# A spectral mixer with soft experts and a gated layer: constants in four pools, weight loads in another order

## The chip, the cores and the metric

The kernel runs on one NeuronCore of one Trainium2 chip. Time is device time in microseconds (us) of one execution; the median of several executions counts. TensorE (PE; its weight loads are PEld), VectorE (DVE), ScalarE (ACT) and GpSimd (POOL) compute; SyncE (SP) only issues transfers. A name with a q behind it (SPq, ACTq) is the engine's queue of instructions. Transfers that are issued by SyncE, ScalarE or GpSimd run on 16 shared DMA engines.

## The reference

All data are float32, with 8 sequences of 3072 tokens and 256 channels.

```python
X = np.fft.rfft(x, axis=1)                       # x: 8 x 3072 x 256
y = np.fft.irfft(X * (filt_r + 1j*filt_i), n=3072, axis=1)
...
logits = y @ phi                                 # y: 24576 x 256; 8 experts x 4 slots
d = softmax over the tokens (axis 0); slot_in = d.T @ y
slot_out[e] = relu(slot_in[e] @ w1[e]) @ w2[e]   # 256 -> 1024 -> 256, per expert
c = softmax over the slots (axis 1);  z = c @ slot_out
...
g = z @ w_gate; v = z @ w_val                    # 256 -> 1536
out = (g * sigmoid(g) * v) @ w_out               # 1536 -> 256
```

## The kernel before, in words

There are three parts, written out in the order in which each engine runs them; nothing reorders the instructions. `phase1` (0 to about 434 us) goes over the 8 sequences in two halves of the channels: a forward transform in two steps (L211, L242), the product with the filter (L250, L251), and for each sequence a `chain` of steps that gets the logits and their token softmax (L346 to L478). It reads four constants from one pool `big`: `ft` (the filter), `inv` and `fwd` (transform matrices) and `nyq`. Beside it `conv` turns the float64 weights of the gated layer, which arrive as integer pairs, into float32 copies in DRAM: `wd[0]` (gate), `wd[1]` (value), `wd[2]` (output). `first_weights` puts the slot softmax of the first sequence's tokens into DRAM as `cd`.

`transition` (about 404 to 469 us) loads expert weights `w1_e` and `w2_e` (1 MB each) and the gate weights `wg` and `wv` (1.5 MB each) into places in SBUF that phase 1 had used. SBUF is full, so each of these loads waits until the tiles whose place it takes have been read for the last time. Places are given back pool by pool. All are issued from SyncE by `flat_load` (L129), in the order of the text; where one waits, those behind it wait too. The expert layer runs as `stage1` (w1, L745, in calls `stage1(0,0)`, `(0,1)`, `(1,0)` and `(1,1)`, where the first index is the half of the experts), transposes `turn` (L762; the copies ht, L763) and `stage2` (w2, L770; first the experts 0 to 3, then 4 to 7). Its output `so` is turned into `sot` and multiplied with wg and wv (L805 for the first 512 columns, L816 for the rest). That gives `g4_0`, `v4_0` and, through `gh` and `gl` and sixteen small transfers (L828), `g4_1`, `g4_2`, `v4_1`, `v4_2`.

`phase2` (from the first G, L916, to the end) goes over 576 items: 8 sequences x 3 x 2 token groups x 12 blocks `f` of 128 of the 1536 columns. An item multiplies the slot softmax `c4` with g4 (G, L916) and v4 (V, L917), forms silu(G)*V, splits it into a high and a low part, and multiplies both with the output weights `wo[f]` (L944, L948), some items later. The first twelve items also split `wo[f]` into two parts (`load_out`, L905, L906). Items f = 0 to 3 use g4_0, items 4 to 7 g4_1. The first `c4` comes from `cd` in four transfers of 384 KB, each to 32 partitions, and `wo` from `wd[2]` in twelve (`first`, L846 and L852), all on SyncE, called after the last `stage1`.

A transfer by SyncE or ScalarE signals its landing on one of eight semaphores that go round. A transfer waits until the one before it on its semaphore has landed, so at most eight of them are under way.

Of the kernel before, what the change touches and what calls it, by code (L numbers as in the profile page):

```python
# [7 lines left out]
F32 = mybir.dt.float32  # L8
F32R = mybir.dt.float32r
# [8 lines left out]
NB, SEQ, D, E = 8, 3072, 256, 32  # L18
NEXP, SPE, FE, FF = 8, 4, 1024, 1536
NJ, NP, NR = 24, 96, 32  # L20
NF = FF // 128
# [58 lines left out]
def spectral_softmoe_glu_kernel(  # L80
# [17 lines left out]
    nc = tc.nc  # L98
# [16 lines left out]
    wd = [dram.tile([256, FF], F32, name="wgd"), dram.tile([256, FF], F32, name="wvd"), dram.tile([FF, 256], F32, name="wod")]  # L115
# [5 lines left out]
    w1s = {}  # L121

    def one(shape, name, stack=c2, side="left", dt=F32):

        p = stack.enter_context(tc.tile_pool(name=f"p_{name}", bufs=1, side=side))
        return p.tile(shape, dt, tag=name, name=name)

    def flat_load(dst, src, p):
        nc.sync.dma_start(out=dst, in_=src.rearrange("(t p) f -> p t f", p=p))  # L129


    def phase1():
        with ExitStack() as c1:
# [6 lines left out]
            yp = [c1.enter_context(tc.tile_pool(name=f"yp{k}", bufs=1)) for k in range(3)]  # L140
            pq = c1.enter_context(tc.tile_pool(name="pq", bufs=2))
            ytp = c1.enter_context(tc.tile_pool(name="ytp", bufs=3))
            big = c1.enter_context(tc.tile_pool(name="big", bufs=1))
            chp = c1.enter_context(tc.tile_pool(name="chp", bufs=1))
            ps_s1 = c1.enter_context(tc.tile_pool(name="ps_s1", bufs=1, space=PSUM))
            ps_x = c1.enter_context(tc.tile_pool(name="ps_x", bufs=2, space=PSUM))
# [1 line left out]
            ps_l = c1.enter_context(tc.tile_pool(name="ps_l", bufs=1, space=PSUM))  # L148
            ps_c = c1.enter_context(tc.tile_pool(name="ps_c", bufs=1, space=PSUM))

            ft = big.tile([128, 12, 2, D], F32, name="ft")
            inv = big.tile([128, NJ, 128], F32, name="inv")
            fwd = big.tile([128, NJ, 128], F32, name="fwd")
            nyq = big.tile([1, D], F32, name="nyq")

            xt = {}
            bt = {}
# [540 lines left out]
    def transition():  # L698
# [5 lines left out]
        w2s = {}  # L704
# [16 lines left out]
        one([128, 2 * D - 64], "pad2")  # L721
        wg = one([128, 2, FF], "wg")
        wv = one([128, 2, FF], "wv")
        flat_load(w2s[0], w2[0], 128)
        for e in range(4, NEXP):
            flat_load(w1s[e], w1[e], 128)
        for e in (1, 2, 3, 5, 6, 7, 4):
            flat_load(w2s[e], w2[e], 128)
        flat_load(wg, wd[0], 128)
        flat_load(wv, wd[1], 128)  # L730

        pool.memset(stm, 0.0)
# [50 lines left out]
        stage1(1, 1)  # L783
        c3.close()
        later = phase2_tiles()
        later["first"]()
        turn(0, 1)
# [14 lines left out]
        for w, dst in gates:  # L802
            pg = bank([128, 512], "h")
            for d_ in range(2):
                pe.matmul(  # L805
                    out=pg, lhsT=sot[:, d_, :], rhs=w[:, d_, 0:512], start=(d_ == 0), stop=(d_ == 1)
# [7 lines left out]
        for d_ in range(2):  # L814
            for i, (w, n, c) in enumerate(parts):
                pe.matmul(  # L816
                    out=pg[32 * i:32 * i + 32, :],
# [8 lines left out]
        for i, (w, n, c) in enumerate(parts):  # L826
            for r in range(4):
                (nc.sync if r < 2 else nc.gpsimd).dma_start(  # L828
                    out=later[n][c][32 * r:32 * r + 32, :].bitcast(F32),
                    in_=(gl if r % 2 else gh)[32 * i:32 * i + 32, :].bitcast(F32),  # L830
# [5 lines left out]
    def phase2_tiles():  # L836
        cp = p2.enter_context(tc.tile_pool(name="cp", bufs=1, side="right"))
        g4 = [cp.tile([128, 512], F32R, name=f"g4_{c}") for c in range(3)]
        v4 = [cp.tile([128, 512], F32R, name=f"v4_{c}") for c in range(3)]
        wo = [cp.tile([128, 2, D], F32R, name=f"wo{f}") for f in range(NF)]  # L840
        c4 = {}

        def first():
            t = cp.tile([128, 3, 2, 512], F32R, tag="c4", name="c4", bufs=2)
            for r in range(4):
                nc.sync.dma_start(  # L846
                    out=t[32 * r:32 * r + 32].rearrange("p q G n -> p q (G n)").bitcast(F32),
                    in_=cd[r // 2].rearrange("q e n -> e q n"),
                )
            c4[0] = t  # L850
            for f in range(NF):
                nc.sync.dma_start(out=wo[f][:, 1, :].bitcast(F32), in_=wd[2][f * 128:(f + 1) * 128, :])  # L852

        def build(b):
            lg = cp.tile([96, E, 32], F32, tag="lg", name="lg", bufs=2)
# [138 lines left out]
    with tc.manual_schedule():  # L994
        phase1()
        phase2(transition())
        p2.close()
# [32 lines left out]
```

## Time and profile before

| | us |
|---|---|
| median of three runs | 1562.45 (1561.62 to 1564.56) |
| profiled execution, whole | 1558.03 |
| its span, first to last instruction | 1556.2 |
| TensorE busy | 1477.5 (95%) |
| VectorE busy | 1182.4 (76%) |
| ScalarE busy | 954.1 (61%) |
| first instruction of phase 2 (L916) | 469.13 |

The page lists engines by busy time and follows the chain of work that ended last back from the last instruction. The timeline gives start, duration, engine, line, operation and tiles, and in brackets how long the engine had been idle and what ended that. A granted clock of 1.0 is TensorE's 2.4 GHz, 0.5 its 1.2 GHz. Buffer numbers are left out of names in the profile: `w` stands for w1_e and w2_e, `c` for c4, `g` and `v` for g4 and v4.

### The profile page before, as it was taken

What the parts mean: (1) busy time and instruction counts of PE and PEld (TensorE: products, weight loads), DVE (VectorE), ACT (ScalarE), POOL (GpSimd) and SP (SyncE); (2) the same over time, 40 slices, a digit from 0 to 9 for tenths busy, and PEclk for the clock granted to TensorE, in tenths of its full rate; (3) what the DMA queues carried; (4) which work ended last, traced back from release to release, by engine and by line L of the source; (5) the groups of instructions that cost most, each with busy time, mean ns of one, the idle gap of its engine ahead of it and who ended that gap; (6) DMA issues with size and microseconds to landing.
All of it is one profiled execution on the core that took longest, in us unless ns stands there. A gap on an engine that the chain in (4) does not pass through costs nothing.

```text
span 1556.2 us, 26502 instructions
## 1 busy us (share of the span) xinstructions
PE 1477.5 (95%) x10218; PEld 1146.6 (74%) x10218; DVE 1182.4 (76%) x1960; ACT 954.1 (61%) x1808; POOL 238.3 (15%) x300
## 2 busy tenths in 40 slices
PE   4799999999778999999999999999999999999998
PEld 1355555555436888888888888888888888888887
DVE  1597887877528887887797788789788878877775
ACT  1365655644316766766776676677667667666665
POOL 0465555553201000000000010000000000000000
PEclk9799999988999999999999999999999999999999
DMA  9997787782592021112102111211211211120111
GB/s 174 181 163 123 131 138 135 128 120 95 206 319 82 14 68 38 28 42 51 28 19 63 38 28 42 51 28 33 50 38 28 62 31 28 35 61 15 27 28 27
DMA packets 105297, 116.58 MB, mean 75 GB/s; under 512 B 14770, under 2 KB 85172, under 8 KB 104916
## 3 DMA queue, kind: packets, MB, share of 16 engines
q1 hardware_dynamic: 102260, 110.44, 33.8%
q10 hardware_dynamic: 2656, 3.93, 0.9%
q8 instruction: 80, 1.31, 0.4%
q0 software_dynamic: 256, 0.52, 0.1%
q14 instruction: 45, 0.37, 0.1%
HBM read 68.21 MB, written 34.60 MB: 66 GB/s over the span
## 4 chain that ended last, share of the span: by engine, by line
PE 84%; DVE 4%; DMA 4%; SPq 3%; ACT 2%; issue 2%; POOL 0%; ACTq 0%; DVEq 0%; POOLq 0%
PE o L944 34%; PE o L948 17%; PE V L917 9%; PE G L916 9%; PE X L242 4%; PE T L273 3%; PE s L211 2%; DMA c<-cd 1%; PE c L455 1%; SPq L173 1%; SPq L129 1%; PE L L282 1%; PE c L417 1%; DMA raw<-in_moe_w_gate_dram 1%; DVE sg L219 1%
## 5 line engine op out<-in xcount | busy, mean ns | idle before, releaser
L944 PE MATMUL o<-wo,hi 128*128 128x512 f32 x2304 | 832.5, 396 | 0.0
L948 PE MATMUL o<-wo,lo 128*128 128x256 f32 x2304 | 646.6, 281 | 0.2 <-DVE lo L933 0.2
L919 ACT ACTIVATE s<-G 128x512 f32<-128x512 f32 x576 | 344.6, 598 | 320.5 <-PE G L916 317.2
L925 DVE TENSOR_TENSOR h<-V,s 128x512 f32<-128x512 f32 x576 | 394.9, 686 | 171.3 <-ACT s L919 168.8
L944 PEld LDWEIGHTS o<-wo,hi 128*128 128x128 f32 x2304 | 433.4, 188 | 102.9
L948 PEld LDWEIGHTS o<-wo,lo 128*128 128x128 f32 x2304 | 435.2, 189 | 25.4 <-DVE lo L933 0.6
L933 DVE TENSOR_TENSOR lo<-h,hi 128x512 fp32r<-128x512 f32 x576 | 417.0, 724 | 0.1
L932 ACT CAST hi<-h 128x512 fp32r<-128x512 f32 x576 | 354.4, 615 | 14.4 <-DVE h L925 10.2
L916 PE MATMUL G<-c,g 128*128 128x512 f32 x576 | 228.4, 397 | 2.2 <-DMA g<-gl 1.6
L917 PE MATMUL V<-c,v 128*128 128x512 f32 x576 | 227.8, 396 | 2.2 <-DVE h L925 1.7
L242 PEld LDWEIGHTS X<-b,fwd 128*64 128x64 f32 x1536 | 86.9, 143 | 76.7 <-issue 51.7
L275 ACT COPY yt<-T 128x512 f32<-128x512 f32 x96 | 55.9, 583 | 136.3 <-PE T L273 132.8
L916 PEld LDWEIGHTS G<-c,g 128*128 128x128 f32 x576 | 108.5, 188 | 28.2 <-issue 3.4
L219 DVE STREAM_TRANSPOSE sg<-s 128x1024 f32<-128x1024 f32 x64 | 79.4, 1240 | 57.2 <-PE s L211 57.0
L242 PE MATMUL X<-b,fwd 128*64 128x128 f32 x1536 | 110.4, 289 | 11.8 <-ACT b L228 10.3
L917 PEld LDWEIGHTS V<-c,v 128*128 128x128 f32 x576 | 109.0, 189 | 4.0 <-DVE h L925 2.8
L863 POOL TENSOR_TENSOR lg<-lg,mx 96x1024 f32<-96x1024 f32 x7 | 16.8, 2397 | 585.4 <-DVE mx L861 585.4
L211 PE MATMUL s<-x,csm 48*64 48x512 f32 x512 | 84.7, 679 | 22.0 <-DMA x<-in_x_dram 15.2
L958 DVE TENSOR_TENSOR ot<-o,tmp 128x256 f32<-128x256 f32 x192 | 70.1, 423 | 38.4 <-ACT tmp L957 38.4
L263 POOL TENSOR_TENSOR y<-P 128x256 f32<-128x256 f32 x96 | 70.2, 732 | 144.7 <-DVE P L250 144.3
L251 DVE TENSOR_TENSOR Q<-X,ft 128x512 f32<-128x512 f32 x96 | 64.9, 677 | 13.7 <-POOL y L263 13.7
L228 ACT COPY b<-sg 128x768 f32<-128x768 f32 x64 | 58.6, 916 | 26.6 <-DVE sg L219 26.3
(194 smaller groups left out, 1021.1 us busy)
## 6 DMA issues: line engine op xcount, KB each, us to landing
x<-in_x_dram SPq DMA_DIRECT2D x64, 384.0 KB, 8.1
out_dram<-ot SPq DMA_DIRECT2D x192, 128.0 KB, 2.2
w<-in_moe_w_dram SPq DMA_DIRECT2D x16, 1024.0 KB, 9.6
c<-ch SPq DMA_DIRECT2D x42, 128.0 KB, 2.4
c<-cl SPq DMA_DIRECT2D x42, 128.0 KB, 2.4
raw<-in_moe_w_gate_dram SPq DMA_DIRECT2D x12, 256.0 KB, 4.5
lgd<-lg ACTq DMA_DIRECT2D x16, 192.0 KB, 4.4
raw<-in_moe_w_val_dram SPq DMA_DIRECT2D x12, 256.0 KB, 3.5
```

Source lines behind the costliest of these rows:

```text
L211: pe.matmul(out=ps[64 * k:64 * k + 64, 16 * r:16 * r + 16, :], lhsT=s1t_sb[64 * r:64 * r + 48, :], rhs=xt[step][64 * r:64 * r + 48, k, :, ...
L219: dve.transpose(out=sg.rearrange("p j d k -> p d j k"), in_=ps.rearrange("p n d -> p d n"))
L242: pe.matmul(out=ps[par * 64:(par + 1) * 64, i, ri, :], lhsT=fwd[:, j, ri * 64:(ri + 1) * 64], rhs=bb[:, j, :],)
L263: pool.tensor_tensor(out=y[:, :, 0, :], in0=P[:, :, 0, :], in1=P[:, :, 1, :], op=ALU.subtract)
L916: pe.matmul(out=pg, lhsT=g4[c][:, fs], rhs=c4[b][:, q, G, :])
L917: pe.matmul(out=pv, lhsT=v4[c][:, fs], rhs=c4[b][:, q, G, :])
L919: act.activation(s, pg, AF.Silu)
L925: dve.tensor_tensor(out=h, in0=pv, in1=s, op=ALU.mult)
L932: act.copy(hi, h)
L933: dve.tensor_tensor(out=lo, in0=h, in1=hi, op=ALU.subtract)
L944: pe.matmul(out=a, lhsT=hi[:, ts], rhs=wo[f].rearrange("p k d -> p (k d)"), start=(f == 0), stop=(f == NF - 1), skip_group_check=True,)
L948: pe.matmul(out=a[:, D:2 * D], lhsT=lo[:, ts], rhs=wo[f][:, 0, :], start=False, stop=(f == NF - 1), skip_group_check=True,)
```

## The change

The four constants get a pool each. The requests of `transition` stand in another order. The first `c4` is requested half by SyncE and half by ScalarE, and `wo` is held in three tiles of four blocks, filled by one transfer each.

```diff
@@ -140,7 +140,7 @@
             yp = [c1.enter_context(tc.tile_pool(name=f"yp{k}", bufs=1)) for k in range(3)]
             pq = c1.enter_context(tc.tile_pool(name="pq", bufs=2))
             ytp = c1.enter_context(tc.tile_pool(name="ytp", bufs=3))
-            big = c1.enter_context(tc.tile_pool(name="big", bufs=1))
+            big = [c1.enter_context(tc.tile_pool(name=f"big{k}", bufs=1)) for k in range(4)]
             chp = c1.enter_context(tc.tile_pool(name="chp", bufs=1))
             ps_s1 = c1.enter_context(tc.tile_pool(name="ps_s1", bufs=1, space=PSUM))
             ps_x = c1.enter_context(tc.tile_pool(name="ps_x", bufs=2, space=PSUM))
@@ -148,10 +148,10 @@
             ps_l = c1.enter_context(tc.tile_pool(name="ps_l", bufs=1, space=PSUM))
             ps_c = c1.enter_context(tc.tile_pool(name="ps_c", bufs=1, space=PSUM))
 
-            ft = big.tile([128, 12, 2, D], F32, name="ft")
-            inv = big.tile([128, NJ, 128], F32, name="inv")
-            fwd = big.tile([128, NJ, 128], F32, name="fwd")
-            nyq = big.tile([1, D], F32, name="nyq")
+            ft = big[0].tile([128, 12, 2, D], F32, name="ft")
+            inv = big[1].tile([128, NJ, 128], F32, name="inv")
+            fwd = big[2].tile([128, NJ, 128], F32, name="fwd")
+            nyq = big[3].tile([1, D], F32, name="nyq")
 
             xt = {}
             bt = {}
@@ -721,12 +721,17 @@
         one([128, 2 * D - 64], "pad2")
         wg = one([128, 2, FF], "wg")
         wv = one([128, 2, FF], "wv")
+
+        for e in (4, 5):
+            flat_load(w1s[e], w1[e], 128)
         flat_load(w2s[0], w2[0], 128)
-        for e in range(4, NEXP):
+        for e in (6, 7):
             flat_load(w1s[e], w1[e], 128)
-        for e in (1, 2, 3, 5, 6, 7, 4):
+        for e in (6, 7):
             flat_load(w2s[e], w2[e], 128)
         flat_load(wg, wd[0], 128)
+        for e in (1, 2, 3, 5, 4):
+            flat_load(w2s[e], w2[e], 128)
         flat_load(wv, wd[1], 128)
 
         pool.memset(stm, 0.0)
@@ -837,19 +842,24 @@
         cp = p2.enter_context(tc.tile_pool(name="cp", bufs=1, side="right"))
         g4 = [cp.tile([128, 512], F32R, name=f"g4_{c}") for c in range(3)]
         v4 = [cp.tile([128, 512], F32R, name=f"v4_{c}") for c in range(3)]
-        wo = [cp.tile([128, 2, D], F32R, name=f"wo{f}") for f in range(NF)]
+        wo4 = [cp.tile([128, 4, 2, D], F32R, name=f"wo{c}") for c in range(3)]
+        wo = [wo4[f // 4][:, f % 4] for f in range(NF)]
         c4 = {}
 
         def first():
             t = cp.tile([128, 3, 2, 512], F32R, tag="c4", name="c4", bufs=2)
+
             for r in range(4):
-                nc.sync.dma_start(
+                (nc.sync if r < 2 else nc.scalar).dma_start(
                     out=t[32 * r:32 * r + 32].rearrange("p q G n -> p q (G n)").bitcast(F32),
                     in_=cd[r // 2].rearrange("q e n -> e q n"),
                 )
             c4[0] = t
-            for f in range(NF):
-                nc.sync.dma_start(out=wo[f][:, 1, :].bitcast(F32), in_=wd[2][f * 128:(f + 1) * 128, :])
+            for c in range(3):
+                nc.sync.dma_start(
+                    out=wo4[c][:, :, 1, :].bitcast(F32),
+                    in_=wd[2][c * 512:(c + 1) * 512, :].rearrange("(f p) d -> p f d", p=128),
+                )
 
         def build(b):
             lg = cp.tile([96, E, 32], F32, tag="lg", name="lg", bufs=2)
```

In the changed file lines behind L721 stand 5 to 10 further down: `flat_load` is still L129, the ht copies are L768, the c4 requests L853, the wo requests L859 and the small transfers L833.

On SyncE, from the load of w1_6 to that of wv. In the kernel before:

```order
L129 DMA w1_6_4734<-in_moe_w1_dram 128x2x1024
L129 DMA w1_7_4730<-in_moe_w1_dram 128x2x1024
L129 DMA w2_1_5083<-in_moe_w2_dram 128x8x256
L129 DMA w2_2_5087<-in_moe_w2_dram 128x8x256
L129 DMA w2_3_5091<-in_moe_w2_dram 128x8x256
L129 DMA w2_5_5135<-in_moe_w2_dram 128x8x256
L129 DMA w2_6_5139<-in_moe_w2_dram 128x8x256
L129 DMA w2_7_5143<-in_moe_w2_dram 128x8x256
L129 DMA w2_4_5131<-in_moe_w2_dram 128x8x256
L129 DMA wg_5155<-wgd_67 128x2x1536
L129 DMA wv_5159<-wvd_68 128x2x1536
```

The same stretch of SyncE in the changed kernel:

```order
L129 DMA w1_6_4743<-in_moe_w1_dram 128x2x1024
L129 DMA w1_7_4739<-in_moe_w1_dram 128x2x1024
L129 DMA w2_6_5151<-in_moe_w2_dram 128x8x256
L129 DMA w2_7_5155<-in_moe_w2_dram 128x8x256
L129 DMA wg_5167<-wgd_67 128x2x1536
L129 DMA w2_1_5095<-in_moe_w2_dram 128x8x256
L129 DMA w2_2_5099<-in_moe_w2_dram 128x8x256
L129 DMA w2_3_5103<-in_moe_w2_dram 128x8x256
L129 DMA w2_5_5147<-in_moe_w2_dram 128x8x256
L129 DMA w2_4_5143<-in_moe_w2_dram 128x8x256
L129 DMA wv_5171<-wvd_68 128x2x1536
```

w2_6, w2_7 and wg moved ahead of w2_1; wv is still last. The load of w2_0, some rows up, moved behind w1_4 and w1_5.

On ScalarE, where the ht copies stand, between `stage1` and `so`. In the kernel before:

```order
L754 ACTIVATE hs0_5075<-h_5180 128x512
L754 ACTIVATE hs1_5079<-h_5200 128x512
L763 COPY ht00_5095<-t_5210 128x512
L763 COPY ht10_5103<-t_5294 128x512
L794 COPY so_5111<-o_5179 128x256
```

The same place on ScalarE in the changed kernel:

```order
L759 ACTIVATE hs0_5087<-h_5192 128x512
L759 ACTIVATE hs1_5091<-h_5212 128x512
L768 COPY ht00_5107<-t_5222 128x512
L853 DMA c4_5258<-cd_71 32x3x1024 x2
L768 COPY ht10_5115<-t_5288 128x512
L799 COPY so_5123<-o_5191 128x256
```

Two of the four c4 requests now stand between the two ht copies.

## Rows read from the trace of the kernel before

**Rows 1.** Page, part 4: shares of the chain that ended last, by engine
```profile
PE 84%; DVE 4%; DMA 4%; SPq 3%; ACT 2%; issue 2%; POOL 0%; ACTq 0%; DVEq 0%; POOLq 0%
```

**Rows 2.** Chain of waits, 426 to 480: start us, us, what
```profile
447.87 21.13 DMA c<-cd
...
473.25 3.53 DMA v<-gl
```

**Rows 3.** SyncE's own waits: who, for whom, us in total, times, longest
```profile
SPq L129 <- PE cl L455: 20.6, 1, 20.6
```

**Rows 4.** SyncE's timeline, 426 to 472: start us, us, line, operation, tiles, count
```profile
426.13 14.81 SPq L129 DMA_DIRECT2D w<-in_moe_w_dram  x7
...
432.13 5.85 SPq L129 DMA_DIRECT2D w<-in_moe_w_dram  x2
...
446.29 2.01 SPq L846 DMA_DIRECT2D c<-cd  x4
...
448.34 6.93 SPq L852 DMA_DIRECT2D wo<-wod  x3
...
462.00 9.22 SPq L852 DMA_DIRECT2D wo<-wod  x9
```

**Rows 5.** Timeline: last readers of the constants ft, inv and fwd
```profile
405.28 0.68 DVE L251 TENSOR_TENSOR Q<-X,ft 128x512 f32<-128x512 f32 x1
...
412.01 0.62 PE L356 MATMUL cl<-inv,lhb 128*32 128x128 f32 x16
...
425.86 1.54 PE L424 MATMUL cl<-fwd,bd 128*32 128x128 f32 x48
```

**Rows 6.** DMA issues: KB each, median us to landing; the last line is L846's
```profile
w<-in_moe_w_dram SPq DMA_DIRECT2D x1, 1024.0 KB, 13.1
...
lgd<-lg ACTq DMA_DIRECT2D x1, 192.0 KB, 7.5
...
DMA to landing us min/median/max: 17.1/19.1/21.1
```

**Rows 7.** Stretches: engines' busy us, granted clock, DMA share, GB/s
```profile
412.00:426.00 14.00, 10.95 (x147) 6.14 (x143) 7.20 (x14) 4.74 (x11) 0.00 (x0) 1.00 0.10 29
...
426.00:448.00 22.00, 20.11 (x268) 9.57 (x261) 5.12 (x17) 4.80 (x11) 0.53 (x1) 1.00 1.00 318
```

**Rows 8.** TensorE's timeline, 441 to 478; in brackets the idle time before
```profile
441.31 1.92 PE L745 MATMUL h<-w,stm 128*32 128x512 f32 x16
...
451.29 3.66 PE L770 MATMUL o<-w,ht 128*32 128x256 f32 x64 [2.56 <-DMA w<-in_moe_w_dram]
...
456.67 1.98 PE L805 MATMUL h<-wg,sot 128*128 128x512 f32 x4 [0.52 <-DVE sot L799]
...
462.03 3.78 PE L805 MATMUL h<-wv,sot 128*128 128x512 f32 x4 [3.38 <-DMA wv<-wvd]
...
465.74 1.06 PE L816 MATMUL t<-wg,sot 128*32 128x512 f32 x1
...
469.13 0.47 PE L916 MATMUL G<-c,g 128*128 128x512 f32 x1 [0.59 <-DMA c<-cd]
...
475.95 0.47 PE L916 MATMUL G<-c,g 128*128 128x512 f32 x1 [1.62 <-DMA g<-gl]
...
476.91 0.47 PE L917 MATMUL V<-c,v 128*128 128x512 f32 x1 [0.50 <-DMA v<-gl]
```

**Rows 9.** Timeline of ScalarE and SyncE at the copies ht, gh and their transfers
```profile
446.31 0.59 ACT L763 COPY ht<-t 128x512 f32<-128x512 f32 x1 [4.31 <-PE t L762]
...
468.62 0.59 ACT L824 CAST gh<-t 128x512 fp32r<-128x512 f32 x1 [2.18 <-PE t L816]
...
471.33 0.58 SPq L828 DMA_DIRECT2D g<-gh  x1
```

**Rows 10.** Stretches at the lower clock: busy us, granted clock, DMA share, GB/s
```profile
461.00:467.00 6.00, 4.97 (x12) 1.57 (x16) 0.54 (x1) 0.58 (x1) 0.00 (x0) 0.50 1.06 206
...
477.80:481.20 3.40, 3.40 (x12) 2.82 (x11) 1.93 (x5) 1.32 (x4) 0.00 (x0) 0.50 0.32 110
```
## Prediction, made before the changed kernel ran

> **What bounds the kernel now.** Read the page's chain first [rows 1]: TensorE carries 84% of the time from the first to the last instruction, so nothing off TensorE's path can be gained or lost except where TensorE stands still. Nearly all of that 84% is phase 2, which the change leaves as it is. The transfers that the change moves all lie between 404 and 477 us, so the second view is the chain in that stretch: it runs through 21.13 us of a c4 transfer and 3.53 us on a piece of v4 [rows 2]. Third is TensorE's timeline there. It idles 2.56 us for expert output weights before stage 2's second half, 3.38 us for wv, 1.62 us and 0.50 us for pieces of g4 and v4 [rows 8]. Fourth is the cause: SyncE, which issues the loads in order, stands 20.6 us on w2_1, whose place becomes free only with a matmul of L455 [rows 3]. Until it ends at 426.13, w2_2 to w2_7, wg and wv stand behind it [rows 4], and the DMA engines are 10% busy over 412 to 426. Over 426 to 448 they are 100% busy [rows 7]. So TensorE waits for transfers that could have run in an idle stretch 14 us long.
>
> **The requests in a new order, with the constants' pools split.** Once split, a load waits only for the last reader of the constant whose place it takes. By the waits of the two built programs w2_6 and w2_7 now wait for ft, read last by the DVE instruction at 405.28 + 0.68; wg for inv, read last at 412.01 + 0.62; wv for fwd, read last at 425.86 + 1.54 [rows 5]. So 1 + 1 + 1.5 MB are asked for at 406 to 413, ahead of the 20.6 us wait. From 426.13 on five w2 loads and wv remain where there were seven, wg and wv. At the 318 GB/s of 426 to 448 [rows 7], which includes the start-up, the 3.67 million bytes are 11.5 us of DMA work, and the 14 idle us hold them. I take them as landed before 426.
>
> What follows on TensorE, step by step:
> (a) Stage 2's second half. The last w2 load is now the fifth in the queue. The fifth before was issued at 432.13 and landed 13.1 us later, at 445.2 [rows 4, 6]. TensorE wants it at 451.29 - 2.56 = 448.7 [rows 8]. The wait goes: 2.6 us.
> (b) wv. The third wo issue, at the end of the 6.93 us from 448.34, stood on wg's landing, 454.9 [rows 4]; wv landed at 462.0 [rows 8], 7.1 us later beside c4. Now wv follows the fifth w2: 445.2 + 7.1 = 452.3 at that pace, 450.1 at 318 GB/s. It is wanted after wg's matmuls, 456.67 - 2.6 + 1.98 = 456.0 [rows 8]. The 3.38 us go.
> (c) The clock. After that wait TensorE was granted 0.50, its 1.2 GHz level, over 461 to 467 [rows 10]. wv's four matmuls took 3.78 us against 1.98 for wg's same four [rows 8]: 1.8 us. From 465.74 to the first G at 469.13 are 3.39 us, for sixteen matmuls in four rounds of four; at wg's 0.5 us a matmul that is 2.0: 1.4 us, which includes the 0.59 us wait for c4. Without the idle stretch I expect 2.4 GHz: 3.2 us. The first G then stands at 469.13 - 2.6 - 3.4 - 3.2 = 459.9.
>
> **c4 on two queues, wo in three transfers.** Four c4 loads go two to SyncE and two to ScalarE. The shortest and the longest landing, 17.1 and 21.1 us after issues 446.29 and about 447.9 [rows 4, 6], put the four at 463.4 to 469.0, so 1.9 us each. Before, wv and c4 together took 454.9 to 469.0, 14.1 us. The latest now is 445.2 + 14.1 = 459.3; the earliest, with both queues at once, 445.2 + 4.9 + 3.75 = 453.9. Both are under the 459.9 that G asks for, so c4 costs and gains nothing by itself, but the slack can be as little as 0.6 us. The Trainium skill speaks against the second queue: "SBUF — State Buffer", section "Can I just issue two DMAs to hit both halves?", says that two transfers at once, at partition 0 and at partition 64, gained only 6% over a single one. By that rule c4 ends near the later bound, and the rival of a late c4 below gets likelier. No row here has two queues on c4.
>
> ScalarE now issues two transfers between two copies ht, and waits for stage 1's last read, 441.31 + 1.92 = 443.2 [rows 8]. It has been idle for 4.31 us when its next copy starts at 446.31 [rows 9]; four issues took SyncE 2.01 us [rows 4], so two are about 1.0 and end near 444.3. Behind them stands only that copy: nothing lost, and 2 us in hand.
>
> wo becomes three requests of 512 KB instead of twelve of 128. Before, nine of the twelve stood on SyncE from 462.00 for 9.22 us, each until an earlier transfer landed [rows 4], so the first g4 piece was issued at 471.33, though gh was ready at 468.62 + 0.59 = 469.2 [rows 9]. Three requests find their turn early. (d) With gh ready at 460.0, the v4 piece that was issued 1.92 us after the first (473.25) goes at 462.0 and lands 3.53 later [rows 2, 9], at 465.6. TensorE is through its first work at 475.95 - 1.62 = 474.3, 5.2 us after the first G, and so now at 465.1; with the next G the V comes at 465.6 [rows 8]. Of 2.1 us idle I take 2.0 as gained. wo's first third has to land by the time its copy follows the first s, about 461; by bytes (1.65 us at 318 GB/s) it lands at 461 at the latest and 455.6 at the earliest. Per third, copies and matmuls are the same, and no reader of one f waits for the copy of another by the order of the built program: nothing.
> (e) Over 477.8 to 481.2, just after those waits, the clock was at 0.50 again with TensorE busy in all 3.40 us [rows 10]. Without the waits I expect full speed: half of it, 1.7 us.
>
> **The rest.** Up to the first expert load every engine has the same rows in the same order, so the four pools cost nothing in phase 1. DMA beside the end of phase 1 is new at 412 to 422; during it TensorE was 78% busy at full clock without it [rows 7]. Bounds for that, plus the two issues on ScalarE: 0 to 1 us lost; I take 0.
>
> Sum: 2.6 + 3.4 + 3.2 + 2.0 + 1.7 = 12.9 us. The profiled execution took 1558.0 us around a span of 1556.2, so 1545.1 by its own time. The median of the runs is 1562.45, 4.4 above the profiled one; I carry that over: **1549.5 us**.
>
> **Rivals.** *wv or c4 late.* The two c4 loads on ScalarE's queue are ahead of wv in time and take engines from it: 2 x 1.9 us on top of 452.3 gives 456.1, at the very point where it is wanted. If the mix costs 2 to 3 us more, TensorE idles about 3 us there and the low clock comes back, 3.2: gain 6.7, 1555.8. Against it: the later bounds already hold the old pace, and c4's share was in it. For it: the old pace was one queue's, and only 0.1 to 0.6 us of slack is left at the later bounds. The skill's rule above, that such transfers serialize, would put c4 there. Chance 0.2.
> *The early requests do not go early.* If the SyncE queue is still held at w2_1's old place, by a full queue or a place that is not free, only c4 and wo remain: (d) and part of (e), 2 to 3 us, 1560. The built order speaks against it. Chance 0.05.
> *Slower.* w2_4 must wait for the store lgd7 from ScalarE, issued at 419 to 420, which now runs beside w2_7 and wg. Another lgd store beside such loads took 7.5 us [rows 6], giving 427.7, under the 432.13 at which w2_4 is due. Each us past 432.13 delays w2_4, wv and c4 alike. At 445 the 12.9 is used up; at 449 the kernel is slower by about 4: 1566. Chance 0.03.
>
> **How the numbers follow.** Forecast 1549.5 with chance 0.7; its own spread comes from (c) to (e): without (e) and half of (c) 1552.8, with full overlap and 0.5 us matmuls at their best 1548. Adding about 1.5 us for how medians differ below gives 1546.5. The range takes the rival of a late wv in: 1546.5 to 1556. Measurements of this kernel can tell 0.2%, 3.1 us, from no change. Faster: forecast, the late wv and 0.02 of the rest, 0.92; the requests that do not go early and small mixtures, 0.05 same; slower 0.03.
>
> **What would show it.** Right: DMA busy over 406 to 422; w2_1 still issued near 426.1; no idle TensorE before stage 2's second half and before wv; the first G near 460 and the granted clock at 1.0 from there; V of the fifth f near 466; no 0.50 stretch between 455 and 490. Wrong: wg landing after 426; TensorE idle for wv or c4; SyncE standing on lgd7's landing; a new low-clock stretch at the start of phase 2; a change in the rows before 404 us or in the pace of phase 2.

## The result, and the profile after

The changed kernel took 1549.29 us, the median of four runs (1547.74 to 1550.86); the kernel before took 1563.43 beside it (1561.62 to 1564.56). The ratio is 0.991, with a 95% interval of 0.9897 to 0.9924: some 14.1 us faster, where 1549.5 (1546.5 to 1556) was predicted. The profiled execution took 1550.86 us, its span 1549.0.

The chain of the page, part 4, shares by engine:

```profile
PE 69%; DVE 0%; ACT 0%; issue 0%
```

It is followed back no further than 471.1 us, hence the 69%. So it does not reach the stretch that the change moves, and that it lacks the 4% of DMA and 3% of SPq of [rows 1] shows nothing; the timelines have to. SyncE's timeline, 404 to 474 (start us, us, line, operation, tiles, count):

```profile
408.40 4.28 SPq L129 DMA_DIRECT2D w<-in_moe_w_dram  x4
...
416.48 0.37 SPq L129 DMA_DIRECT2D wg<-wgd  x1
...
431.34 8.67 SPq L129 DMA_DIRECT2D w<-in_moe_w_dram  x5
...
440.10 3.33 SPq L129 DMA_DIRECT2D wv<-wvd  x1
...
448.55 0.82 SPq L853 DMA_DIRECT2D c<-cd  x2
...
449.42 6.81 SPq L859 DMA_DIRECT2D wo<-wod  x3
...
465.49 0.58 SPq L833 DMA_DIRECT2D g<-gh  x1
```

The longest of SyncE's own waits (total us, times, longest):

```profile
SPq L129 <- PE cl L455: 14.4, 1, 14.4
```

w1_6, w1_7, w2_6 and w2_7 are the x4 at 408.40, and wg goes at 416.48. The last readers of ft and inv, as in [rows 5], now read:

```profile
409.08 0.68 DVE L251 TENSOR_TENSOR Q<-X,ft 128x512 f32<-128x512 f32 x1
...
415.80 0.62 PE L356 MATMUL cl<-inv,lhb 128*32 128x128 f32 x16
```

They end at 409.76 and 416.42, so wg goes as soon as inv's place is free, and w2_6 and w2_7 go within the x4, which is over at 412.7. Only then does SyncE stand on w2_1, now 14.4 us and with less behind it; [rows 3] had 20.6. wo is out at 456.2, nine microseconds before SyncE has a piece to send, where [rows 4] had it busy with wo until 471.2. The stretches that answer to [rows 7] (engines' busy us, granted clock, DMA share, GB/s):

```profile
411.00:427.00 16.00, 11.87 (x153) 7.14 (x157) 7.03 (x15) 5.99 (x14) 0.00 (x0) 0.92 0.98 363
...
431.00:453.00 22.00, 20.10 (x272) 9.70 (x264) 5.11 (x17) 4.81 (x11) 0.00 (x0) 1.00 0.98 322
```

The early requests keep DMA 98% busy over 411 to 427. In the 14 us before w2_1 goes out it is 67% busy (417.2 to 431.2) where [rows 7] had 10%: wg has landed by 427.4, and the rest is still idle. Issues by form, 404 to 480 (KB each, median us to landing):

```profile
wg<-wgd SPq DMA_DIRECT2D x1, 1536.0 KB, 10.9
...
wv<-wvd SPq DMA_DIRECT2D x1, 1536.0 KB, 16.7
```

The landings of the four c4 transfers, from the view of that tile:

```profile
DMA to landing us min/median/max: 8.5/11.2/12.5
```

So wg landed at 427.4, wv at 440.10 + 16.7 = 456.8, and c4 between 448.5 + 8.5 = 457.0 and 448.95 + 12.5 = 461.5. TensorE, 424 to 472 (in brackets the idle time before):

```profile
424.99 3.34 PE L455 MATMUL cl<-y,dh 128*32 128x256 f32 x32 [1.41 <-ACT dh L328]
...
440.65 5.36 PE L750 MATMUL h<-w,stm 128*32 128x512 f32 x48 [0.39 <-DVE stm L742]
...
453.87 3.66 PE L775 MATMUL o<-w,ht 128*32 128x256 f32 x64
...
459.25 1.98 PE L810 MATMUL h<-wg,sot 128*128 128x512 f32 x4 [0.52 <-DVE sot L804]
...
461.07 1.88 PE L810 MATMUL h<-wv,sot 128*128 128x512 f32 x4
...
464.74 0.50 PE L926 MATMUL G<-c,g 128*128 128x512 f32 x1
...
469.98 0.39 PE L926 MATMUL G<-c,g 128*128 128x512 f32 x1
...
471.23 0.47 PE L927 MATMUL V<-c,v 128*128 128x512 f32 x1 [0.86 <-DVE wo L916]
```

Beside [rows 8]: no wait stands before stage 2's second half, before wv or before the first G, and wv's matmuls take 1.88 us instead of 3.78. The one wait of that size left is 0.86 us before V of the fifth item. The row puts it down to VectorE's part of wo, but by the built program this V waits for the four pieces of v4_1 and an earlier h, not for wo, and in two profiles further down the same place reads `DMA v<-gl`. Half of the sixteen pieces are issued by GpSimd; here the last piece of v4_1 was one of those, asked for at 467.76 and landed 3.3 us later, at 471.0. The first line, at the end of phase 1, is slower than in before (3.34 us against 1.93); it comes back in the last experiment.

For all that follows, the time is cut at four instructions of the trace: the last read of ft (DVE L251), the first matmul of stage 1, the first G, and V of the fifth item.

| us | ft to stage 1 | stage 1 to first G | first G to fifth V | fifth V to the end | median of runs |
|---|---|---|---|---|---|
| before | 30.16 | 33.69 | 7.78 | 1079.3 | 1563.4 |
| after | 31.57 | 24.09 | 6.49 | 1077.8 | 1549.3 |

### The profile page after: what moved, and what is told of

Its sections match the earlier page's. It is cut to its first block, busy times and chain, and to the rows that moved or that the text cites. A ratio compares the mean times of both kernels' runs of the same rounds, so it can differ in the third digit from the quotient of the medians.

```text
span 1549.0 us, 26487 instructions
## 1 busy us (share of the span) xinstructions
PE 1473.9 (95%) x10218; PEld 1143.6 (74%) x10218; DVE 1183.7 (76%) x1960; ACT 955.1 (62%) x1808; POOL 239.2 (15%) x300
## 4 chain that ended last, share of the span: by engine, by line
PE 69%; DVE 0%; ACT 0%; issue 0%
PE o L954 34%; PE o L958 17%; PE V L927 9%; PE G L926 9%; DVE wo L916 0%; DVE ot L968 0%; ACT s L929 0%; DVE lo L943 0%; DVE h L935 0%; ACT hi L942 0%; ACT tmp L967 0%; ACT wo L915 0%
## 5 line engine op out<-in xcount | busy, mean ns | idle before, releaser
L942 ACT CAST hi<-h 128x512 fp32r<-128x512 f32 x576 | 354.7, 616 | 14.5 <-DVE h L935 10.2
L242 PE MATMUL X<-b,fwd 128*64 128x128 f32 x1536 | 110.0, 288 | 12.5 <-ACT b L228 10.3
L211 PE MATMUL s<-x,csm 48*64 48x512 f32 x512 | 83.8, 666 | 21.3 <-DMA x<-in_x_dram 14.1
L251 DVE TENSOR_TENSOR Q<-X,ft 128x512 f32<-128x512 f32 x96 | 64.9, 676 | 14.5 <-POOL y L263 14.5
L273 PE MATMUL T<-csm,y 128*128 128x128 f32 x384 | 64.8, 292 | 11.4 <-POOL y L263 5.5
```

Of the source, the lines that this page charges most:

```text
L211: pe.matmul(out=ps[64 * k:64 * k + 64, 16 * r:16 * r + 16, :], lhsT=s1t_sb[64 * r:64 * r + 48, :], rhs=xt[step][64 * r:64 * r + 48, k, :, ...
L242: pe.matmul(out=ps[par * 64:(par + 1) * 64, i, ri, :], lhsT=fwd[:, j, ri * 64:(ri + 1) * 64], rhs=bb[:, j, :],)
L942: act.copy(hi, h)
```

## Experiments on the parts

**The changed kernel again.** No edit.

> The changed kernel once more, unchanged, beside the kernel before: it tells what of the 14.1 us between the two medians is the change, and what is how one execution differs from another. Theory: the change is worth the three terms that the profile after shows in the transition, 9.6 + 1.3 + 1.5 = 12.4 us, so before minus after comes out at 12.4, give or take 1; the stretch before 404 us wanders by some us from execution to execution in either kernel, with stretches at a granted clock of 0.5 at changing places. Rival: the four pools gain something in the stretch before 404 us; then that stretch is shorter in every execution of the changed kernel, and before minus after is 14 or more.

Median 1548.97 us (1544.5 to 1556.08, six runs) against 1563.14 for before; ratio 0.9911 (0.9889 to 0.9933). The stretches were 31.50, 24.08, 6.70 and 1078.1 us: phase 2 and the transition repeat to 0.3 us. The difference is 14.2, outside the theory's 12.4 give or take 1, and where the rival had put it. But the rival's stretch is not shorter: ft's last read stands at 405.3 to 408.5 us in the three profiles of before (two are taken further down) and at 406.0 to 410.3 in the ten of kernels with four pools. What the 14.2 are comes out of the last experiment.

**c4 and wo as before, c4 as before, wo as before.** From the changed kernel, in turn: both edits undone as in the diff below, the first alone, the second alone.

```diff
...
-                (nc.sync if r < 2 else nc.scalar).dma_start(
+                nc.sync.dma_start(
...
-            for c in range(3):
-                nc.sync.dma_start(
-                    out=wo4[c][:, :, 1, :].bitcast(F32),
...
+            for f in range(NF):
+                nc.sync.dma_start(out=wo[f][:, 1, :].bitcast(F32), in_=wd[2][f * 128:(f + 1) * 128, :])
```

> The four pools and the new order of the requests alone; c4 on SyncE's queue and wo in twelve transfers, as in the kernel before. Theory: terms (a), (b), (c) and (e) stay, (d) goes: nine wo requests hold SyncE while gh is ready, so TensorE waits 1.3 to 2.0 us for the pieces of g4 and v4 at the fifth item: 1550.6 to 1551.3. Rival 1: c4 on one queue lands after the first G wants it (464.7 in the profile after), up to 3.75 us late: 1551 to 1555, with TensorE idle at the first G. Rival 2: c4 and wo are worth nothing because the transfers are early anyway: 1549.3.

> The changed kernel with all four c4 requests back on SyncE; the pools, the order and wo in three are kept. Theory: c4 costs and gains nothing by itself: it lands by 462 to 464 after wv, before the first G, 1549.3 give or take 0.7. Rival 1: the two queues overlap, and without them c4 lands 2 to 3.75 us later, after the first G wants it: 1550.5 to 1552.5. Rival 2: the two c4 requests on ScalarE cost time, by delaying wv or the copy ht: 1548 or less.

> The changed kernel with wo back in twelve transfers of 128 KB; the pools, the order and c4 on two queues are kept. Theory: the twelve requests hold SyncE past the time when gh is ready (465.5 in the profile after), each until an earlier transfer has landed; the first g4 piece goes out 1.5 to 3 us later, and TensorE waits for pieces at the fifth item: 1550.6 to 1551.3. Rival: the transfers ahead now land early enough that SyncE is through its wo requests before 465: 1549.3 give or take 0.7.

| us | stage 1 to first G | first G to fifth V | fifth V to the end | median (runs) | ratio to before |
|---|---|---|---|---|---|
| both undone | 24.08 | 6.90 | 1078.0 | 1551.42 (5) | 0.9923 (0.9907 to 0.9939) |
| c4 on one queue | 24.08 | 6.75 | 1078.0 | 1549.28 (4) | 0.9909 (0.9892 to 0.9926) |
| wo in twelve | 24.09 | 5.93 | 1078.0 | 1550.38 (5) | 0.9903 (0.9885 to 0.9922) |

Neither edit can be told from nothing: the stretches differ from those of the changed kernel by 0.8 us at most and the intervals overlap. For c4 that was expected, and rival 1 falls. For wo it was not: of the 1.5 to 3 us for which twelve requests were to hold SyncE, 0.8 us are left with both undone and none with wo alone. That the time with both undone, 1551.42 us, is near the 1550.6 to 1551.3 of its theory does not bear the theory out, since from stage 1 to the end it takes 1108.9 us, the changed kernel 1108.4 and 1108.8. SyncE's timeline with both undone:

```profile
447.70 15.82 SPq L858 DMA_DIRECT2D wo<-wod  x12
...
463.62 0.58 SPq L833 DMA_DIRECT2D g<-gh  x1
```

TensorE's, at the first G and the fifth V:

```profile
462.08 0.50 PE L922 MATMUL G<-c,g 128*128 128x512 f32 x1
...
468.99 0.47 PE L923 MATMUL V<-c,v 128*128 128x512 f32 x1 [1.26 <-DMA v<-gl]
```

The twelve requests are out at 463.52, the first piece goes at 463.62, 1.5 us after the first G; in the changed kernel it went 0.75 us after it. They still stand one behind the other, but what they stand on lands earlier. So the early requests alone had all but emptied SyncE's queue. With wo in twelve and c4 on two queues the first piece again goes 0.75 us after the first G (465.33 and 464.58), and the same V waits 0.30 us:

```profile
470.52 0.47 PE L923 MATMUL V<-c,v 128*128 128x512 f32 x1 [0.30 <-DMA v<-gl]
```

With c4 on one queue its landings read:

```profile
DMA to landing us min/median/max: 9.8/12.0/14.1
```

From the first issue at 449.28 and the last at about 450.6 that is 459.1 to 464.7, 1.9 us each, and the first G stood at 465.47: 0.8 us in hand. On two queues the last landed 20.8 us after the start of stage 1, on one 23.3. The Trainium skill ("SBUF — State Buffer", section "Can I just issue two DMAs to hit both halves?") has two transfers at once gain only 6%. Of these four, two queues saved 2.5 us out of some 7.5 (four times 1.9), so here the measurement differs from the rule.

## Experiments on the pools and the order

**One pool, new order**, and **four pools, old order**, both with c4 and wo as changed:

```diff
-            big = [c1.enter_context(tc.tile_pool(name=f"big{k}", bufs=1)) for k in range(4)]
+            big = c1.enter_context(tc.tile_pool(name="big", bufs=1))
...
-            ft = big[0].tile([128, 12, 2, D], F32, name="ft")
+            ft = big.tile([128, 12, 2, D], F32, name="ft")
...
```

```diff
...
-        for e in (6, 7):
-            flat_load(w2s[e], w2[e], 128)
         flat_load(wg, wd[0], 128)
...
-        for e in (1, 2, 3, 5, 4):
+        for e in (1, 2, 3, 5, 6, 7, 4):
             flat_load(w2s[e], w2[e], 128)
```

> The changed kernel with the four constants back in one pool. By the waits of the built program w2_6, the first of the moved requests, now waits for the last reader of the whole pool, a matmul of L424 that ended at 427.40 in the profile of before. Theory: the stretch from 412 to 426 stays idle, all transfers start some 1.3 us later than before the change, and in an order that puts w2_1 to w2_3 behind 3.67 million bytes: TensorE waits some 2 to 3 us in each half of stage 2, the first G comes at 464.5 to 469 by before's clock, and of the gain some 2 us from g4 and v4 pieces and up to 5 us more are left: 1556 to 1561. Rival: the gain comes from the order itself and not from the places that come free early: within 1 us of 1549.3.

> The changed kernel with the expert and gate weights requested in the order of before; the four pools, c4 on two queues and wo in three are kept. Theory: SyncE stands some 20 us on w2_1 as before, the waits for w2_5 and the like and for wv stay, and only (d) and part of (e) are gained, less what two c4 requests on ScalarE, now ahead of wv, take from wv (up to 3.75 us): 1559.5 to 1563. Rival: the split pools alone bring the loads forward: 1556 or less.

With one pool 1561.44 us (twelve runs), ratio 0.9987 (0.9974 to 1.0); with the old order 1560.75 (twelve), 0.9984 (0.9971 to 0.9996); before beside them 1564.1. So 2.7 and 3.4 us of the 14 are left, and in both kernels c4 and wo are as changed. The rivals, 1549.3 without the split pools and 1556 or less without the order, fall. One pool, SyncE's longest wait:

```profile
SPq L129 <- PE cl L424: 22.7, 1, 22.7
```

One pool, TensorE's timeline in stage 2 and at wv's matmuls:

```profile
451.10 0.62 PE L775 MATMUL o<-w,ht 128*32 128x256 f32 x2 [2.39 <-DMA w<-in_moe_w_dram]
...
457.91 3.26 PE L775 MATMUL o<-w,ht 128*32 128x256 f32 x26 [6.19 <-DMA w<-in_moe_w_dram]
...
471.34 1.88 PE L810 MATMUL h<-wv,sot 128*128 128x512 f32 x4
```

The new order now stands 22.7 us on the pool's last reader, and stage 2's first half waits for w2_2 and w2_3, because w2_6, w2_7 and wg are ahead of them. Stage 1 to the first G takes 35.55 us. The theory had 29 to 33.6; what it left out, c4 on ScalarE's queue, shows next (here two of the c4 transfers go at 447.3 and 447.7, and the first landed at 454.5, ahead of w2_3 at 457.9). Old order, TensorE's timeline at stage 2's second half and the first G:

```profile
458.14 6.41 PE L771 MATMUL o<-w,ht 128*32 128x256 f32 x64 [6.40 <-issue]
...
472.37 0.47 PE L922 MATMUL G<-c,g 128*128 128x512 f32 x1 [0.28 <-DVE v L811]
```

Old order, issues by form, 404 to 480:

```profile
c<-cd ACTq DMA_DIRECT2D x2, 384.0 KB, 7.9
...
wv<-wvd SPq DMA_DIRECT2D x1, 1536.0 KB, 20.0
```

Old order, the landings of the four c4 transfers:

```profile
DMA to landing us min/median/max: 7.1/14.2/20.6
```

Here stage 2's second half waits 6.40 us where [rows 8] had 2.56: ScalarE's c4, asked for at 446.3 and 446.7, landed at 454.4 in the mean, ahead of the last w2 load, which was asked for at 441.1. The granted clock is 0.50 from 456.9 to 463.7, and its matmuls take 6.41 us instead of 3.66. And yet stage 1 to the first G is 33.91, as before: the last c4, on SyncE's queue, was asked for at 451.6 and landed at 472.1, and the first G follows it at 472.37. The other two stretches are 6.53 and 1077.9, as in the changed kernel. So c4 and wo as changed are worth about 2.6 us in the old order by the first profile of before, and 3.4 us by the runs, as (d) and (e); beside the early requests nothing of it can be told from zero: two cures for the same wait.

**wg not early.**

```diff
-        flat_load(wg, wd[0], 128)
         for e in (1, 2, 3, 5, 4):
             flat_load(w2s[e], w2[e], 128)
+        flat_load(wg, wd[0], 128)
```

> The changed kernel with wg requested where it stood before, after the w2 loads, so that only w2_6 and w2_7 use the idle stretch: 2.1 of the 3.67 million bytes. It asks whether the gain follows the bytes. Theory: wg's 1.57 million bytes come back behind the five w2 loads; at 318 to 418 GB/s that is 3.8 to 4.9 us more for wv and c4, which had 4.2 and 3.3 us in hand. So wv is just late (0 to 1 us), c4 lands 0.5 to 1.6 us after the first G wants it, and the low clock may come back for a while: from stage 1 to the first G 24.6 to 27 us instead of 24.08, 1550 to 1552.5 in all. Rival: any transfer left behind the wait costs its whole length, 1553 to 1554; or two loads are enough, 24.1 us.

1556.29 us (nine runs), ratio 0.9958 (0.9941 to 0.9976), 7 us above the changed kernel; stage 1 to the first G 29.17 us. The theory by bytes falls: it allowed 27 and 1552.5. Its rivals, 24.1 us or 1553 to 1554, fall too. TensorE at wv's matmuls:

```profile
464.54 2.83 PE L810 MATMUL h<-wv,sot 128*128 128x512 f32 x4 [3.18 <-DMA wv<-wvd]
```

Issues by form, 404 to 480:

```profile
c<-cd ACTq DMA_DIRECT2D x2, 384.0 KB, 10.8
...
wv<-wvd SPq DMA_DIRECT2D x1, 1536.0 KB, 21.2
```

wv lands at 443.28 + 21.2 = 464.5, 23.7 us after the start of stage 1 instead of 16.2. Of the 7.5 us, 3.8 to 4.9 are wg's bytes at the rates of the expectation. The rest fits the two c4 transfers on ScalarE: asked for at 448.6, 5.4 us after wv, they landed at 459.6 in the mean (10.8), ahead of it. At 1.5 to 1.9 us each they are 3 to 3.8; no run has wg late and c4 on one queue, so this share is reckoned, not shown. The Trainium skill ("DMA: Bandwidth & Descriptors", section "Queues, rings and completion order") has the DMA engines take turns between the queues; the landings here agree. What was in hand (4.2 us) is used up, 3.18 of waiting follow, and a slower wv (2.83 us) after it.

## Experiments on the clock

**wv behind c4 and wo**, so that it is late again; then the wait **filled** with nine matmuls on wg that nobody reads, and with five.

```diff
-        flat_load(wv, wd[1], 128)
...
         later["first"]()
+        flat_load(wv, wd[1], 128)
```

```diff
         for w, dst in gates:
+            if w is wv:
+                pf = bank([128, 512], "h")
+                for k in range(9):
+                    pe.matmul(out=pf, lhsT=sot[:, k % 2, :], rhs=wg[:, k % 2, 0:512])
             pg = bank([128, 512], "h")
```

> The changed kernel with one request moved: wv behind c4 and wo, so that it lands late and TensorE has to wait for it as in the kernel before. It prices the clock. Theory (terms (c) and (e)): wv lands at 464.5 to 466, TensorE idles 3.5 to 5 us before its matmuls, the granted clock falls to 0.5, wv's four matmuls take 3.6 to 3.8 us instead of 1.9, the sixteen of the next line 3 us instead of 1.9, and some microseconds at 0.5 follow in the first items: 1549.3 + 3.5 to 5 + 3.2 + 1.7 = 1557.7 to 1559.2. Rival: the idle time is all it costs: 1552.8 to 1554.3.

> As the kernel with wv behind c4 and wo, and with nine matmuls of wg's own operands, into a bank that nobody reads, put where TensorE waits for wv (some 4.5 us at 0.5 us each). Wv lands at the same time, but TensorE is busy while it waits. Theory: the clock stays at 1.0, the 3.2 and the 1.7 us are not paid: 3 to 5 us under the kernel without them, 1552.8 to 1555. Rival: the clock has other reasons, or the slow matmuls come from the transfers beside them: as without the nine, 1557 to 1559, or slower by what of the nine does not fit.

> As the kernel with wv behind c4 and wo and nine filling matmuls, with five of them: each took 0.88 us there (eighteen instructions in 7.89 us), so nine overran the wait of 4.36 us by 3.5 us and five just fill it. Theory: wv's matmuls take 1.9 us, the sixteen behind them 1.9, and from the start of stage 1 to the first G are 28.5 to 28.9 us, against 31.01 with the wait unfilled and 24.08 where nothing is late: the clock is worth 2.2 to 2.5 us; 1553.5 to 1555 by the time. Rival: 31 us and 1557, the filling changes nothing.

| us | stage 1 to first G | first G to fifth V | fifth V to the end | median (runs) | ratio to before |
|---|---|---|---|---|---|
| wv last | 31.01 | 6.50 | 1078.0 | 1557.48 (12) | 0.9958 (0.9946 to 0.9971) |
| nine matmuls | 31.81 | 6.56 | 1078.1 | 1556.82 (7) | 0.9959 (0.9943 to 0.9976) |
| five matmuls | 28.73 | 6.72 | 1078.0 | 1556.20 (12) | 0.9955 (0.9941 to 0.9969) |

wv last, TensorE's timeline:

```profile
465.02 3.78 PE L810 MATMUL h<-wv,sot 128*128 128x512 f32 x4 [4.36 <-DMA wv<-wvd]
...
468.74 1.06 PE L821 MATMUL t<-wg,sot 128*32 128x512 f32 x1
```

wv last, the stretch of the low clock (columns as in [rows 7]):

```profile
463.00:469.80 6.80, 4.78 (x12) 1.58 (x16) 0.34 (x1) 0.58 (x1) 0.00 (x0) 0.50 0.01 5
```

Five matmuls, TensorE's timeline at the filling and at wv:

```profile
463.71 4.45 PE L811 MATMUL h<-wg,sot 128*128 128x512 f32 x10
...
468.28 1.95 PE L814 MATMUL h<-wv,sot 128*128 128x512 f32 x4
```

After 4.36 us of idling the granted clock was 0.50, TensorE's 1.2 GHz, over 463.0 to 469.8 and the same matmuls took twice as long. With the wait filled by five it stayed at 1.00 (455 to 475) and they took 1.95 us. From the start of stage 1 to the first G that is 31.01 against 28.73: the clock costs 2.3 us here, as the theory of the five had it. Nine overran the wait: they took 7.89 us, since each is two instructions of 0.44 us, which I had overlooked. The times alone do not tell 2.3 us: the ratios, 0.9958 and 0.9955, have overlapping intervals, and with the wait filled both times, 1556.82 and 1556.20, lie above what was expected (1552.8 to 1555 and 1553.5 to 1555). One part of the theory fell: wv last has no low clock after the first G, and 1078.0 us to the end, so the 1.7 us of (e) do not follow from a wait before wv.

## Two more profiles of the kernel before

No edit.

> The kernel before, once more, for a second profile of it. Two things hang on it. First: in all eight profiles of kernels with the new order the granted clock is 0.5 for 3.4 to 6.8 us from 15 to 16 us after ft's last read, which makes the end of phase 1 1.3 to 2.8 us longer (31.4 to 33.0 us from ft's last read to stage 1, against 30.16 in the profile of before and in that of the old order). Theory: this comes and goes from execution to execution and is no cost of the new order: it is seen in some executions of before too (31.4 or more). Rival: it belongs to the new order; then before shows 30.16 again. Second: in the first profile of before the clock was 0.50 over 477.8 to 481.2, and the stretch from V of the fifth item to the end was 1079.29 us against 1077.8 to 1078.1 in all eight others. Theory (term (e)): this follows the waits for pieces of g4 and v4, so that before shows about 1079.3 again. Rival: chance; then 1078.0 can come out.

> The kernel before a third time, for one more profile, with the same two questions: 30.16 or at least 31.4 us from ft's last read to stage 1, and 1079.3 or 1078.0 us from V of the fifth item to the end.

| us | ft to stage 1 | stage 1 to first G | first G to fifth V | fifth V to the end | run |
|---|---|---|---|---|---|
| before, again | 31.59 | 34.38 | 10.14 | 1079.6 | 1564.97 |
| before, third | 31.83 | 34.54 | 9.89 | 1080.0 | 1566.53 |

The second profile of before, TensorE's timeline:

```profile
454.91 3.66 PE L770 MATMUL o<-w,ht 128*32 128x256 f32 x64 [2.66 <-DMA w<-in_moe_w_dram]
...
464.36 1.98 PE L805 MATMUL h<-wv,sot 128*128 128x512 f32 x4 [2.09 <-DMA wv<-wvd]
...
473.34 0.77 PE L916 MATMUL G<-c,g 128*128 128x512 f32 x1 [5.15 <-DMA wo<-wod]
...
482.90 0.76 PE L916 MATMUL G<-c,g 128*128 128x512 f32 x1 [4.09 <-DMA g<-gl]
```

The same, the landings of the four c4 transfers:

```profile
DMA to landing us min/median/max: 16.3/18.4/21.6
```

The third profile of before, the first G:

```profile
474.86 0.77 PE L916 MATMUL G<-c,g 128*128 128x512 f32 x1 [5.24 <-DMA wo<-wod]
```

The second profile again, SyncE's timeline:

```profile
452.04 24.42 SPq L852 DMA_DIRECT2D wo<-wod  x12
...
476.88 0.58 SPq L828 DMA_DIRECT2D g<-gh  x1
```

The same, two stretches (columns as in [rows 7]):

```profile
470.60:477.40 6.80, 4.06 (x9) 2.49 (x10) 2.63 (x6) 3.25 (x8) 3.00 (x7) 0.50 1.00 190
...
480.80:487.70 6.90, 4.80 (x13) 3.87 (x14) 1.62 (x3) 1.83 (x4) 0.00 (x0) 0.51 0.45 118
```

Compare [rows 8]. wv's wait is 2.09 us and its matmuls run at full speed, and yet the first G comes later, after 5.15 us of idling. The row names wo; by the built program this G waits for c4, of which the last piece was asked for at 451.6 and landed 21.6 us later, at 473.2. wo then holds SyncE until 476.46, so the fifth G waits 4.09 us for its piece. The granted clock is at 0.50 after each of the two waits. The profile that the prediction was made from was a mild case of the same thing.

Three answers follow. Term (e) is real: 1079.3 to 1080.0 in three profiles of before, which have a low clock there, 1077.8 to 1078.1 in all eleven others, which have none; no run took the low clock away by itself. The slower end of phase 1 (31.4 us and more) is not owed to the early transfers alone: before shows it in two of three profiles, and so does one pool, whose transfers are not early. Whether they make it more frequent stays open: it is there in nine of nine profiles with them and in three of five without. And the gain from stage 1 to the end is 12.4 us by the two first profiles, but 1124.3 - 1108.6 = 15.7 by the others of before against the mean of the two of the changed kernel; over all three profiles of before 14.5, which agrees with the 14.1 us of the runs.

## Why the prediction was right, point by point

The cause on record, transfers that wait in order behind w2_1 while DMA idles, was right. That the forecast lies within 0.3 us of the median is luck: several terms were off by more and made up for one another, as the points show.

- *What bounded the kernel* was right: transfers that stood behind w2_1 while DMA idled. The rival in which the early requests do not go early had forecast 2 to 3 us for c4 and wo alone; one pool and the old order gave 2.7 and 3.4.
- *(a)*, 2.6 us: right. The wait is gone; the two other profiles of before have 2.66 and 2.39.
- *(b) and (c)*, 6.6 us: the sum is right, with (a) 9.2 forecast and 33.69 - 24.09 = 9.6 measured, but the step is not. It gave wv's wait and the slow clock a price each, as if the first G followed from them. In all three profiles of before the first G waited for c4's landing (0.59, 5.15 and 5.24 us); the waits for w2 and wv and the low clock filled time that TensorE would have idled anyway. In the old order stage 2 ended 6.6 us later than in before, counted from stage 1, and the first G came only 0.2 us later. What set the end was c4, at the end of the queue of transfers; this is read from four profiles, and no run moved all of c4 forward alone. The 3.2 us for the clock even hold the 0.59 us wait for c4. The sum held because in the changed kernel c4 lands before TensorE is through, as the step on c4 had it (by 0.6 us at the least), so that TensorE's path sets the first G there. The clock has a price of its own only where nothing else is late: 2.3 us in the experiment with wv last.
- *c4 on two queues gains nothing by itself*: right. Its slack at the later bound was put at 0.6 us; on one queue 0.8 was measured, on two 3.3.
- *(d)*, 2.0 us: 1.3 against the first profile of before, 3.2 to 3.7 against the other two. The credit was wrong: wo in three transfers was to free SyncE, but twelve hold it for 0.8 us at most once the loads ahead land early. The 0.7 us that were missing beside the first profile come for the most part from one offset: gh was put 0.1 us after the first G, as in before, where the first G had itself waited 0.59 us for c4. Now it is ready 0.7 us after it. The rest is that GpSimd's last piece landed 0.2 us after SyncE's, and the step had reckoned with SyncE's alone.
- *(e)*, 1.7 us: 1.5 to the first profile, 1.6 to 2.1 with the others.
- *The end of phase 1*, 0 to 1 us taken as 0: right as far as can be told. It took 1.4 us more than in the first profile of before (31.57 against 30.16), but no more than in the other two (31.59 and 31.83). TensorE's rows agree within 0.02 us up to a matmul 15.9 us after ft's last read, with transfers beside them or without.
- *From the span to the median*: 4.4 us were carried over as if the change left them alone. Part of it was phase 1 (stage 1 began at 435.44 in that execution, at 438.96 and 440.32 in the other two), but 3.4 to 3.6 us lay in the stretch that the change shortens. So the gain was put at 12.9 where 14.1 was measured, and the base at 1562.45 where the runs beside the changed kernel gave 1563.4; the two nearly cancel.
- *The rival of a late wv or c4* did not come about: wv landed 4.2 us before its matmuls, c4 3.3 us before the first G. Its mechanism, ScalarE's c4 passing older requests, shows where loads are late: by the reckoning above some 3 us of wv's landing with wg not early, and a longer wait before stage 2 in the old order, though there not a later first G. *The slower rival* never came near: the stores lgd7 landed by 428.2, and w2_4 went at 437.3.
- *The signs set down beforehand*: w2_1, the first G and V of the fifth item came 5 us after their places (431.34, 464.74 and 471.23 for 426.1, 460 and 466), because stage 1 began at 440.65 instead of 435.44. Counted from stage 1 all three are right within 0.5 us. Two of the signs of being wrong did show by the letter: wg landed at 427.4, after 426, but 3.9 us before w2_1's request, and the rows before 404 us came later. That last shift is one between executions: ft's last read, 3.8 us later here, wanders by 3.2 us among the three profiles of before and by 4.3 among the ten with four pools. The clock stayed at 1.0 from 427.9 on.

## What to carry to other kernels

Where a queue in program order stands on one late buffer, look for requests behind it whose places come free earlier, and check what a pool makes them wait for: here the split pools without the new order, or the order without the pools, did not bring the first G forward (33.9 and 35.6 us after stage 1, against 33.7 to 34.5). Before adding up several waits in a row, ask which transfer is last in the queue behind all of them, since its landing bounds what can be gained. A request on a second queue landed ahead of older ones here, so it should be one that is needed sooner than those.

## What the chip showed beside this

- In twelve of the fourteen profiles the granted clock fell to 0.50 at the same place near the end of phase 1, 14.8 to 16.0 us after ft's last read, and cost 1.3 to 2.8 us. In the first profile of before and in that of the old order it did not, although TensorE's rows ahead of that place agree to 0.02 us. What decides it stays open. The Trainium skill ("TensorE: Matmul & The Clock Gate", section "What's actually happening") has the window behind the clock gate run free of the kernel's start, by which the same work could meet it at another point in each execution; the starts, spread over 1.2 us, fit that, but no run here sets the point. Second profile of before:

```profile
422.80:426.20 3.40, 2.93 (x28) 1.36 (x32) 1.29 (x3) 1.73 (x4) 0.00 (x0) 0.50 0.21 64
```

- Single runs of one kernel differ by more than the terms argued about: the changed kernel ran from 1544.5 to 1556.1 us. One profile is then a poor base for terms of 1 to 3 us; two more of before changed the gain to explain from 12.4 to 14.5.
